# Turning a weight matrix by DMA instead of by TensorE, and one group later

## The chip, the cores and the metric

The kernel runs on one core of a Trainium2 chip. Times are microseconds (us) of device time for one whole execution. The core has TensorE (PE, matrix products and their weight loads), VectorE (DVE), ScalarE (ACT), GpSimd (POOL) and SyncE (SP), each with its own stream of instructions that it runs in order, and 16 DMA engines that all queues share. In this kernel POOL issues the loads and most of the stores, and SP issues the DMA transposes.

## What is computed

```python
def _attn_ref(u, v, z):                    # u, v: 8 x 3072 x 256; z: 8 x 3072 x 64
    scores = (1.0 / S) * np.matmul(z, z.transpose(0, 2, 1))
    attn = np.maximum(scores, 0.0) ** 2
    return u * np.matmul(attn, v)

def _moe_ref(x, w1, w2, w_out):            # w1, w2: 256 x 1024; w_out: 1024 x 256
    g = np.maximum(x @ w1, x @ w2)
    return g @ w_out
```

The second function is applied to the first one's result. Two identities shape the kernel. The score matrix is symmetric, so a block right of the diagonal, turned, is the block left of it. And max(a, b) = max(a - b, 0) + b, so `g @ w_out = relu(x @ (w1 - w2)) @ w_out + x @ (w2 @ w_out)`: the kernel prepares `w15 = w1 - w2` and `W2o = w2 @ w_out` once, and then needs only one wide product, one ReLU and one narrow product for each group.

## The kernel before

**Tiles and groups.** A batch's 3072 rows are 24 tiles of 128; four tiles make a group, six groups a batch. A block is the squared ReLU of the scores of one group against another: 512 x 512 in bf16, held as 128 x 2048 (512 KB) in one of 28 slots (`Block`). A free slot carries a tick from which it counts as free; `release(after=COOL)` sets it 40 ticks on. Scores are made in pairs (`score_pair`): two PE matmuls, two ReLUs out of PSUM (`r_sb`, lines 221 and 223) and a squaring on DVE (lines 229, 231), two pairs to a block. The pairs are numbered in one list. Of batch 0, pairs 0 to 11 are group 0's, 12 to 21 group 1's, 22 to 29 group 2's, 30 to 35 group 3's. For the pairs below 22, every third one gives its second ReLU to DVE rather than ACT.

**Mirrors.** The block (batch, group, block column) right of the diagonal is turned by a DMA transpose on SP (`mirror`, line 262). Most are issued as soon as the block is squared; six of batch 0 go to a list `later` and are issued at set places in groups 1, 2 and 3. SP also turns u (`turn_u`, line 186) and z (`turn_z`, line 142). All of these go through one queue in the order in which the program emits them.

**The start: four plain groups.** Groups 0 to 3 of batch 0 are worked through one by one (the loop over `i`). Each goes over 24 tiles `n` and two halves of v's columns `dc`, two matmuls each (line 278), which is one slot and one tick. At the head of groups 1 to 3 (6, 6 and 9 tiles) and at the tail of groups 0 to 2 (6, 6 and 9) the tiles are taken for one `dc` first and then for the other, else both in turn. New score pairs are emitted every fourth slot (`pair_slots`), ahead of their use. Inside the loop, with `dc` 0, stand the other steps of the start, each at its own `(i, n)`: adding the two halves of the previous group's sums (line 629, groups 1 and 2), its gates (`gate`, line 423: the product with u, times the scale), loading w2, w1 and w_out by POOL (line 646), the later mirrors, and u's and z's transposes.

Into this loop the weights' preparation is laid. At tile 16 of group 2, DVE subtracts `w15`, and PE turns w2 in 16 transposes of 128 x 128 (line 658) into two PSUM tiles, which ACT copies to `w2T_sb` (line 661). At the end of group 2, sixteen matmuls make W2o (line 673), which ACT copies (line 680). PSUM tiles tagged "mm" have four buffers, shared by scores, these products and the feed-forward. `w1`, `w2` and `w2T` lie in three of the 28 slots until they are released.

**After the start.** The sums of group 3 are drained (ACT copies, line 295, and DVE adds, line 297). Then the feed-forward (`ff`) runs for groups 0 and 1: `d_ps` with w15 (line 439), ReLU on ACT (446), `o_ps` first with W2o (453), then with w_out (462). From there couples of groups alternate with the feed-forward of the couple before; couple 2 (groups 4 and 5) uses the mirrored blocks of batch 0, in the order of block columns 4, 5, 2, 3, 0, 1. From batch 1 on, a form with seven instead of eight products is used (line 894), which the change doesn't touch. The schedule is manual: each engine runs its instructions in the order in which the program emits them, and waits are put in where data or a buffer need them.

Of the kernel before, what the change touches and what calls it, by code (L numbers as in the profile page):

```python
# [11 lines left out]
def kernel(  # L12
# [10 lines left out]
    nc = tc.nc  # L23
    fp32 = mybir.dt.float32
    bf16 = mybir.dt.bfloat16
# [7 lines left out]
    P = 128  # L33
# [6 lines left out]
    KD = D // P  # L40
    KF = Dff // P
# [7 lines left out]
    COOL = 40  # L49
# [14 lines left out]
    mm_psum = ctx.enter_context(tc.tile_pool(name="mm_psum", bufs=4, space=bass.MemoryType.PSUM))  # L64
# [56 lines left out]
    def zT_pe(lo, n, engine):  # L121
        tp = mm_psum.tile([P, n, P], bf16, name="tpz", tag="mm")
        for j in range(n):
            nc.tensor.transpose(
                tp[:, j, :], zd_first(lo + j, 1).rearrange("p t h d -> p (t h d)"), ident
            )
        copy = nc.scalar.copy if engine == "act" else nc.vector.tensor_copy
        copy(zT[:, lo : lo + n, :], tp)  # L128
# [144 lines left out]
    def attn_unit(b, g, t, acc, dc, first, last):  # L273
        blk, j = divmod(t, G)
        a = A[b, g, blk]
        for half in range(2):
            rows = ds(half * R, R)
            nc.tensor.matmul(  # L278
                a.out(acc[half, dc]),
                v_at(b, t, dc)[rows],  # L280
                a.moving(rows, j),
                start=first,
                stop=last,
            )
        if dc == KD - 1 and j == G - 1:
            a.release()
# [4 lines left out]
    def drain(acc, dcs):  # L291
        hs = {}
        for dc in dcs:
            hs[dc] = new_h()
            nc.scalar.copy(hs[dc], acc[1, dc])
        for dc in dcs:
            nc.vector.tensor_add(hs[dc], hs[dc], acc[0, dc])
        return hs

    def drain_fast(acc, dc):  # L300
        hs = [new_h() for half in range(2)]
        nc.scalar.copy(hs[1], acc[1, dc])
        nc.vector.tensor_copy(hs[0], acc[0, dc])
        return hs
# [172 lines left out]
    ident = consts.tile([P, P], bf16)  # L477
# [28 lines left out]
    done = 0  # L506
    due = []

    def emit_pair(wait=0):
        nonlocal done  # L510
        early = done < 22
        finish = score_pair(
            *pairs[done], dve_half=1 if early and done % 3 == 0 else None, halves=done == 0
        )
        done += 1
        if wait:
            due.append((tick + wait, finish))
        else:
            finish()
# [10 lines left out]
    def steps_of(i):  # L530
        tiles, both = range(NT), range(KD)
        head = edge(i - 1) if i else 0
        tail = NT - edge(i)
        steps = [(n, dc) for dc in both for n in tiles[:head]]
        steps += [(n, dc) for n in tiles[head:tail] for dc in both]
        return steps + [(n, dc) for dc in both for n in tiles[tail:]]

    def pair_slots(i):
        return (
            [1, 3] + list(range(6, 40, 4)),  # L540
            list(range(3, 41, 4)),
            list(range(3, 41, 4)),
            list(range(0, 44, 4)),
        )[i]

    def need(b, g, n):
        most = pair_at[b, g, 2 * g]
        for t in range(n + 1):
            if t // G >= g:
                most = max(most, pair_at[b, g, t // 2] + 1)  # L550
        return most

    with tc.manual_schedule():
# [14 lines left out]
        w1, w2, w2T = Block(), Block(), Block()  # L568
        w1_sb, w2_sb = (w.ap.rearrange("p (c f) -> p c f", c=KD) for w in (w1, w2))
        w2T_sb = w2T.ap.rearrange("p (c k r) -> p c k r", c=KD, r=P)  # L570

        def new_acc():
            return {
                (half, dc): acc_tile(2 * half + dc) for half in range(2) for dc in range(KD)
            }
# [26 lines left out]
        sums = None  # L602
        for i in range(PLAIN):
            b, g = groups[i]
            if i:
                acc = new_acc()
            new, slots = {}, pair_slots(i)
            for slot, (n, dc) in enumerate(steps_of(i)):
                tick += 1
                k = need(b, g, n)  # L610
                upto = max(k, min(done + 1, k + AHEAD)) if slot in slots else k
                while done < min(upto, len(pairs)):
                    emit_pair()
                if i == 0 and slot in (10, 22):
                    zT_pe(12 if slot == 10 else 20, 8 if slot == 10 else 4, "act")
                    if slot == 22:
                        for x in z_first:
                            x.release()
                attn_unit(b, g, n, acc, dc, n == 0, n == NT - 1)
                if n == NT - 1 and i < PLAIN - 1:  # L620
                    if i < 2:
                        new[dc] = drain_fast(acc, dc)
                    else:
                        new.update(drain(acc, [dc]))
                if dc:
                    continue
                if i in (1, 2) and n in (6, 8):
                    halves = sums[n // 2 - 3]
                    nc.vector.tensor_add(halves[0], *halves)
                    sums[n // 2 - 3] = halves[0]  # L630
                if i and n == 10:
                    gates = gate(*groups[i - 1], sums)
                if i and n in (10, 12):
                    gates.pop(0)()
                if i == 0 and n == 14:
                    turn_u(0, 0)
                if i + 1 < PLAIN:
                    if i and n == 1:
                        load_u(*groups[i + 1])
                    if n == (13 if i == 2 else 16):  # L640
                        turn_u(*groups[i + 1])
                if (i, n) in ((0, 20), (1, 10)):
                    w_in = ((w2_sb, moe_w2), (w1_sb, moe_w1)) if i == 0 else ((w_out_sb, moe_w_out),)
                    nc.vector.memset(w_in[0][0][:, 0, 0:1], 0.0)
                    for w_sb, w in w_in:
                        nc.gpsimd.dma_start(
                            out=w_sb, in_=w.rearrange("(c p) f -> p c f", p=P)
                        )
                if later and n % 4 == 0 and (i == 3 or i and n > 12):
                    later.sort(key=lambda block: block[2])  # L650
                    mirror(*later.pop(0))
                if i == 2 and n == 16:
                    nc.vector.tensor_sub(w15_sb, w1_sb, w2_sb)
                    w1.release()
                    for dc in range(KD):
                        tp = mm_psum.tile([P, KF, P], bf16, name="tpw", tag="mm")
                        for j in range(KF):
                            nc.tensor.transpose(  # L658
                                tp[:, j, :], w2_sb[:, dc, ts(j, P)], ident
                            )  # L660
                        nc.scalar.copy(w2T_sb[:, dc, :, :], tp)
                    w2.release()
                if (i, n) in ((1, 16), (2, 14)):
                    load_z(1, i - 1, held=True)
                if (i, n) == (2, 8):
                    turn_z(1, 0)
                if (i, n) == (3, 14):
                    load_z(1, 2, held=True)
            if i == 2:
                for dc in range(KD):  # L670
                    ps = mm_psum.tile([P, D], fp32, name="w2o_ps", tag="mm")
                    for nb in range(KF):
                        nc.tensor.matmul(  # L673
                            ps,
                            w2T_sb[:, dc, nb, :],
                            w_out_sb[:, nb, :],
                            start=(nb == 0),
                            stop=(nb == KF - 1),
                        )
                    nc.scalar.copy(W2o_sb[:, dc, :], ps)  # L680
                w2T.release()
            sums = new
        sums = None
# [47 lines left out]
        sums = drain(acc, range(KD))  # L731
# [10 lines left out]
        for i in range(PLAIN // 2, len(couples)):  # L742
# [129 lines left out]
            for s, pair in enumerate(steps):  # L872
                while halves_done and halves_done[0][0] <= s:
                    _, name, mm = halves_done.pop(0)
# [13 lines left out]
                for half, (name, w, blk, j) in enumerate(pair):  # L888
                    rows = ds(half * R, R)
                    if name not in acc:  # L890
# [3 lines left out]
                    mm = nc.tensor.matmul(  # L894
                        a.out(acc[name]),
                        w()[rows],
                        a.moving(rows, j),
                        start=name not in opened,
                        stop=left[name] == 0,
                    )  # L900
# [57 lines left out]
```

## Time and profile before

| | us |
|---|---|
| median of 9 runs (lowest, highest) | 911.86 (911.1, 924.36) |
| the profiled execution: its time | 911.63 |
| its span on the core | 909.9 |
| PE busy | 899.1 |
| DVE busy | 724.7 |
| ACT busy | 602.8 |
| POOL busy | 105.6 |
| group 2, by PE's timeline | about 37 to 51.7 |
| group 3, by PE's timeline | 53.55 to 66.4 |
| first feed-forward starts | 66.39 |

The lines of a timeline begin with the start and the duration in us, then engine, line of the kernel, operation, the tiles written and read, their shape, the number of instructions put together in the line, and in brackets the idle time before it and what ended that. "SPq" is SP's queue, where the duration is that of the issue; the landing of a DMA is told apart. Busy PE time counts pipelined matmuls, each 0.2 us behind the next in the steady state, so that durations of single matmuls overlap.

### The profile page before, as it was taken

What the parts mean: (1) busy time and instruction counts of PE and PEld (TensorE: products, weight loads), DVE (VectorE), ACT (ScalarE), POOL (GpSimd) and SP (SyncE); (2) the same over time, 40 slices, a digit from 0 to 9 for tenths busy, and PEclk for the clock granted to TensorE, in tenths of its full rate; (3) what the DMA queues carried; (4) which work ended last, traced back from release to release, by engine and by line L of the source; (5) the groups of instructions that cost most, each with busy time, mean ns of one, the idle gap of its engine ahead of it and who ended that gap; (6) DMA issues with size and microseconds to landing.
All of it is one profiled execution on the core that took longest, in us unless ns stands there. A gap on an engine that the chain in (4) does not pass through costs nothing.

```text
span 909.9 us, 19258 instructions
## 1 busy us (share of the span) xinstructions
PE 899.1 (99%) x7494; PEld 518.4 (57%) x7542; DVE 724.7 (80%) x1095; ACT 602.8 (66%) x1191; POOL 105.6 (12%) x199
## 2 busy tenths in 40 slices
PE   8999999999999999999999999999999999999998
PEld 4456465565565555665646656566465564655655
DVE  6772789779998799887997979978799788995640
ACT  6797966667666676667676666666766567673445
POOL 3101010111110101101011012010110110100000
PEclk9999999999999999999999999999999999999999
DMA  9999999999799896999769999799998999888201
GB/s 186 164 203 211 151 167 173 173 179 171 135 184 182 151 185 115 203 173 168 155 118 214 168 149 173 145 177 150 188 172 141 166 174 184 154 158 147 74 25 70
DMA packets 379500, 145.08 MB, mean 159 GB/s; under 512 B 358160, under 2 KB 362640, under 8 KB 379408
## 3 DMA queue, kind: packets, MB, share of 16 engines
q1 hardware_dynamic: 356960, 91.27, 62.6%
q0 software_dynamic: 22448, 52.57, 30.8%
q8 instruction: 59, 0.97, 0.5%
q14 instruction: 33, 0.27, 0.1%
HBM read 59.77 MB, written 25.17 MB: 93 GB/s over the span
## 4 chain that ended last, share of the span: by engine, by line
PE 97%; DVE 1%; DMA 1%; issue 1%; ACT 0%; ACTq 0%; DVEq 0%; POOLq 0%
PE acc L894 45%; PE o_ps L462 18%; PE d_ps L439 18%; PE s_ps L210 7%; PE o_ps L453 5%; PE acc L278 4%; DMA v_sb<-in_v_dram 1%; DVE blk L231 1%; ACT r_sb L223 0%; PE w2o_ps L673 0%; DVE r_sb L221 0%; ACT zT L128 0%; PE tpw L658 0%; DVE xT L423 0%; ACT o_sb L474 0%
## 5 line engine op out<-in xcount | busy, mean ns | idle before, releaser
L894 PE MATMUL acc<-blk,v_sb 64*128 64x512 bf16 x2208 | 450.4, 376 | 0.0
L223 ACT ACTIVATE r_sb<-s_ps 128x512 bf16<-128x512 f32 (+3 forms) x668 | 334.2, 559 | 122.0 <-PE s_ps L210 78.6
L894 PE MATMUL acc<-blk,vt 64*128 64x512 bf16 x1512 | 364.1, 376 | 0.0
L894 PEld LDWEIGHTS <-v_sb 64*128 64x128 bf16 x2208 | 176.2, 94 | 134.9 <-issue 5.9
L231 DVE TENSOR_TENSOR blk<-r_sb 128x1024 bf16<-128x1024 bf16 x257 | 172.6, 689 | 90.0 <-ACT r_sb L223 89.0
L446 ACT ACTIVATE g_sb<-d_ps 128x512 bf16<-128x512 f32 x384 | 193.3, 630 | 28.2 <-PE acc L894 17.8
L462 PE MATMUL o_ps<-w_out_sb,g_sb 128*128 128x256 bf16 x1536 | 175.5, 273 | 0.0
L894 PEld LDWEIGHTS <-vt 64*128 64x128 bf16 x1512 | 139.2, 94 | 62.4
L439 PE MATMUL d_ps<-xT,w_sb 128*128 128x512 bf16 x720 | 167.6, 379 | 2.6 <-issue 0.2
L462 PEld LDWEIGHTS <-g_sb 128*128 128x128 bf16 x1536 | 150.3, 98 | 17.4
L474 ACT COPY o_sb<-o_ps 128x512 f32<-128x512 f32 (+1 forms) x98 | 56.3, 577 | 132.4 <-PE o_ps L462 132.4
L769 DVE TENSOR_TENSOR h_sb<-h_sb,acc 128x512 f32<-128x512 f32 x168 | 109.4, 682 | 27.7 <-ACT h_sb L773 20.3
L210 PE MATMUL s_ps<-zT 64*128 64x512 bf16 (+3 forms) x676 | 125.8, 357 | 0.6 <-ACT zT L128 0.4
L439 PEld LDWEIGHTS <-w_sb 128*128 128x128 bf16 x768 | 73.2, 98 | 89.7 <-issue 9.9
L475 POOL DMA_DIRECT2D out_dram<-o_sb x88 | 48.1, 546 | 543.8 <-ACT o_sb L474 543.8
L330 DVE TENSOR_TENSOR blk<-blk,blk 128x2048 bf16<-128x2048 bf16 x63 | 76.8, 1219 | 3.7 <-DMA blk<-blk 3.7
L334 DVE TENSOR_TENSOR blk<-blk,blk 128x2048 bf16<-128x2048 bf16 x63 | 77.2, 1225 | 2.2
L784 DVE TENSOR_TENSOR blk<-blk,blk 128x2048 bf16<-128x2048 bf16 x63 | 76.6, 1218 | 0.0
L338 DVE TENSOR_TENSOR blk<-blk,blk 128x2048 bf16<-128x2048 bf16 x63 | 73.4, 1219 | 0.9 <-DMA blk<-blk 0.9
L423 DVE SCALAR_TENSOR_TENSOR xT<-h_sb,uT 128x512 bf16<-128x512 f32 x96 | 62.0, 684 | 3.8 <-PE o_ps L453 3.8
L229 DVE TENSOR_TENSOR blk<-r_sb 128x512 bf16<-128x512 bf16 (+3 forms) x162 | 46.3, 323 | 20.1 <-ACT r_sb L223 19.1
L210 PEld LDWEIGHTS <-zT 64*128 64x128 bf16 x676 | 35.6, 94 | 38.1 <-ACT zT L128 0.9
(50 smaller groups left out, 320.9 us busy)
## 6 DMA issues: line engine op xcount, KB each, us to landing
out_dram<-o_sb POOLq DMA_DIRECT2D x88, 256.0 KB, 3.9
un<-in_u_dram POOLq DMA_DIRECT2D x48, 256.0 KB, 5.8
v_sb<-in_v_dram POOLq DMA_DIRECT2D x21, 512.0 KB, 7.4
blk<-blk SPq DMA_TRANSPOSE x239, 5.0
zn<-in_z_dram POOLq DMA_DIRECT2D x21, 128.0 KB, 4.3
v_sb<-in_v_dram POOLq DMA_DIRECT2D x6, 256.0 KB, 7.6
out_dram<-o_sb SPq DMA_DIRECT2D x6, 256.0 KB, 2.0
blk<-in_moe_w_dram POOLq DMA_DIRECT2D x2, 512.0 KB, 6.5
```

The lines of the kernel that those rows point to most:

```text
L210: nc.tensor.matmul(s_ps[h][:, lo[h] :], zT[rows, z_at(b, blk * G + tiles[h]), :], zT[rows, q + lo[h] // P : q + G, :].rearrange("p t c -> ...
L223: nc.scalar.activation(o, s, AF.Relu)
L231: nc.vector.tensor_mul(a[:, k : k + 2, :], r, r)
L330: nc.vector.tensor_add(*alike(f["S1"], f["A21"], f["A22"]))
L334: nc.vector.tensor_sub(*alike(f["S2"], f["S1"], f["A11"]))
L338: nc.vector.tensor_sub(*alike(f["S3"], f["A11"], f["A21"]))
L439: nc.tensor.matmul(d_ps, w15_sb[:, kc, ts(nb, P)], xT[:, kc, :], start=(kc == 0), stop=(kc == KD - 1),)
L446: nc.scalar.activation(g_sb[:, nb, :], d_ps, AF.Relu)
L462: nc.tensor.matmul(o_ps[t // 2][:, t % 2, :], g_sb[:, nb, ts(t, P)], w_out_sb[:, nb, :], start=False, stop=(nb == KF - 1 and t % 2 == 1),)
L769: nc.vector.tensor_add(out, a, b_)
L784: nc.vector.tensor_sub(f["A12"].ap, f["A12"].ap, f["S2"].ap)
L894: mm = nc.tensor.matmul(a.out(acc[name]), w()[rows], a.moving(rows, j), start=name not in opened, stop=left[name] == 0,)
```

## The change

1. `early` covers pairs below 12 rather than below 22: pairs 12, 15, 18 and 21 give both their ReLUs to ACT.
2. In groups 1 and 2 the first add of halves moves from tile 6 to tile 5, the gates from tiles 10 and 12 to tiles 11 and 14 (groups 1 to 3).
3. The 16 PE transposes of w2 and their two ACT copies at tile 16 of group 2 are gone. In their place SP issues one DMA transpose of the whole w2 at tile 2 of group 3. w2's slot is released there, with 40 ticks to wait, and w2T's one group later.
4. W2o's matmuls and copies stand at the end of group 3 rather than of group 2.

```diff
     def emit_pair(wait=0):
         nonlocal done
-        early = done < 22
+        early = done < 12
...
-                if i in (1, 2) and n in (6, 8):
-                    halves = sums[n // 2 - 3]
-                    nc.vector.tensor_add(halves[0], *halves)
-                    sums[n // 2 - 3] = halves[0]
-                if i and n == 10:
+                if i in (1, 2) and n in (5, 8):
+                    k = n // 8
+                    nc.vector.tensor_add(sums[k][0], *sums[k])
+                    sums[k] = sums[k][0]
+                if i and n == 11:
                     gates = gate(*groups[i - 1], sums)
-                if i and n in (10, 12):
+                if i and n in (11, 14):
                     gates.pop(0)()
...
                 if i == 2 and n == 16:
                     nc.vector.tensor_sub(w15_sb, w1_sb, w2_sb)
                     w1.release()
-                    for dc in range(KD):
-                        tp = mm_psum.tile([P, KF, P], bf16, name="tpw", tag="mm")
-                        for j in range(KF):
-                            nc.tensor.transpose(
-                                tp[:, j, :], w2_sb[:, dc, ts(j, P)], ident
-                            )
-                        nc.scalar.copy(w2T_sb[:, dc, :, :], tp)
-                    w2.release()
+                if (i, n) == (3, 2):
+                    nc.sync.dma_start_transpose(
+                        w2T.ap.rearrange("p (k r) -> p k r", r=P), w2.ap
+                    )
+                    w2.release(after=COOL)
...
-            if i == 2:
+            if i == 3:
                 for dc in range(KD):
                     ps = mm_psum.tile([P, D], fp32, name="w2o_ps", tag="mm")
                     for nb in range(KF):
```

## The prediction

> **What bounds the kernel now.** I read the page first: the busy time of the engines and the chain that ended last.
>
> ```profile
> PE 899.1 (99%) x7494; PEld 518.4 (57%) x7542; DVE 724.7 (80%) x1095; ACT 602.8 (66%) x1191; POOL 105.6 (12%) x199
> PE 97%; DVE 1%; DMA 1%; issue 1%; ACT 0%; ACTq 0%; DVEq 0%; POOLq 0%
> ```
>
> TensorE (PE) is busy for 99% of the span, and 97% of the chain is PE. So a microsecond taken from PE's sequence is gained, one in which PE waits is lost, and other engines count only where PE waits for them. The change lies in the first 80 us, so I next read PE's part of the timeline there (start, duration, engine, line).
>
> ```profile
> 1.19 2.53 PE L581 MATMUL acc<-blk 128*128 128x512 bf16 x7 [1.19 <-DVE blk L557]
> ...
> 32.14 0.37 PE L210 MATMUL s_ps<-zT 64*128 64x512 bf16 x1 [0.20 <-DVE r_sb L221]
> ...
> 32.94 0.82 PE L278 MATMUL acc<-blk,v_sb 64*128 64x512 bf16 x6 [0.21 <-DVE blk L231]
> ...
> 36.15 2.55 PE L278 MATMUL acc<-blk,v_sb 64*128 64x512 bf16 x22 [0.58 <-DVE blk L231]
> ...
> 46.62 1.07 PE L658 MATMUL tpw<-ident,blk 128*128 128x128 bf16 x16
> 47.62 0.82 PE L278 MATMUL acc<-blk,v_sb 64*128 64x512 bf16 x6
> ...
> 51.70 1.92 PE L673 MATMUL w2o_ps<-w_out_sb,blk 128*128 128x256 bf16 x16
> 53.55 0.39 PE L210 MATMUL s_ps<-zT 64*128 64x512 bf16 x2
> ...
> 66.39 3.63 PE L439 MATMUL d_ps<-xT,w_sb 128*128 128x512 bf16 x15
> ```
>
> The 16 transposes hold PE from 46.62 to 47.62 us, 1.00 us; W2o from 51.70 to 53.55, 1.85 us; the first feed-forward starts at 66.39. Group 1 has three waits for VectorE (DVE), 0.20 + 0.21 + 0.58 us.
>
> The new transpose goes through SP's queue, so I read that queue's timeline over groups 2 and 3, then the landing times of its seven L262 transposes issued between 55 and 73 us.
>
> ```profile
> 51.43 2.58 SPq L262 DMA_TRANSPOSE blk<-blk  x1
> 54.11 1.25 SPq L186 DMA_TRANSPOSE uT<-un  x1
> 55.46 18.74 SPq L262 DMA_TRANSPOSE blk<-blk  x7
> 74.30 4.50 SPq L142 DMA_TRANSPOSE zT<-zd  x2
> ```
>
> ```profile
> 65.79 8.41 SPq L262 DMA_TRANSPOSE blk<-blk  x3
> ```
>
> ```profile
> L262 SPq DMA_TRANSPOSE blk<-blk x7: 1809/2341/3511, 55.5 to 71.3; - x7
> DMA to landing us min/median/max: 4.6/5.7/6.2
> ```
>
> SP has no gap: each issue begins where the last one ends, from 51.43 to 78.80 us, at 1.81 to 3.51 us a block. The queue is late. By the program the last seven mirrors are, in order: (0,2,5), (0,0,4), (0,1,4) from group 2, then (0,3,4), (0,0,5), (0,1,5), (0,3,5) from group 3. So (0,0,5), which the program emits at the first tile of group 3 (PE about 53.6 us), is issued only at 65.79: 12 us behind PE. Nobody waits for these seven before couple 2 (groups 4 and 5, after 82 us), so the lag costs nothing today.
>
> **The change part by part.**
>
> *Four ReLUs move.* Pairs 12, 15, 18 and 21 lose their DVE half: 4 x 0.685 us (L221) off DVE, 4 x 0.597 us (L223) onto ScalarE (ACT). From 21.3 to 36.2 us ACT is busy 10.4 of 14.9 us, so 2.4 more fits. With the first add at slot 5 instead of 12 and the gates at slots 22 and 28 instead of 20 and 24, DVE has less to do where PE waits. This takes up to 0.99 us of waits and, where PE's eight-matmul runs stretch from 1.04 to 1.17, 1.17 and 1.34 us, up to 0.56: between 0 and 1.55 us earlier at the end of group 1. I take 1.0. The late gate adds one wait: u's transpose for group 3 is emitted at tile 13 of group 2 and reuses the buffer that the gate at tile 14 still reads. SP comes to it at 54.11, DVE to that gate near 47, so it is free by 7 us; otherwise all of SP's queue would stand behind it.
>
> *The PE transposes go.* PE gets 1.00 us and ACT two copies of 1.03 us, which cost nothing on the path.
>
> *W2o moves* from the end of group 2 to that of group 3: the 16 matmuls and their weight loads keep their 1.85 us and only change place. Its two ACT copies (0.37 us each) now stand ahead of group 3's two drains (0.58 each), which stand ahead of the first feed-forward ReLU. That ReLU starts some 1.5 us after the d_ps matmuls instead of 0.85; with four PSUM buffers at 0.43 us of PE each, the fifth matmul group waits: 0 to 0.8 us, I take 0.6.
>
> *The DMA transpose of w2* is one more instruction in SP's queue, of the size of a block (128 x 2048 bf16, 512 KB), emitted at tile 2 of group 3: after (0,3,4) and (0,0,5), ahead of (0,1,5) and (0,3,5). For those behind it, it costs one more issue, 1.8 to 3.5 us; (0,3,5), now landed at 77.5, and the two z transposes, ended at 78.8, have that room before couple 2. The POOL queue is not touched. w2's and w2T's blocks stay taken for some tens of slots more; the plan has nine or more free through group 3, so no mirror is delayed for lack of one.
>
> But W2o needs it. PE reaches W2o at 66.39 - 1.00 - 1.85 - 1.0 = 62.5 us, and runs in program order: the feed-forward stands behind it. SP reaches the transpose where it now reaches (0,1,5): 65.79 + 3.5 = 69.3 us. The shorter DVE work lets SP start its unbroken run at most 0.6 us sooner, from u's transpose at 33.51, so 68.7. Landing is 4.6 to 6.2 us later in the rows; of those issued from 61 to 66 us it is 4.6, 5.2 and 4.8, and I take 4.8: **w2T lands at 73.5 us, and PE stands idle for 11 us.**
>
> Bounds of the landing: with every mirror from 51.43 on at the fastest issue, 51.43 + 6 x 1.81 + 1.25 + 0.6 (gaps) = 64.2, landed at 68.8; with every one at the slowest, 51.43 + 6 x 3.51 + 1.85 = 74.3, landed at 80.5. The middle rows decide, because this is the same queue in the same stretch.
>
> *PE after the pause.* The first row of PE's timeline shows that PE starts slowly: seven matmuls (five of 512 columns, two of 128) take 2.53 us, where the later rate, 15 of 512 in 3.63, would give about 1.3. This slow rate ends within some 3.3 us of work. Whether 11 us of rest brings it back no row shows: the longest later idle, 0.98 us, does not. So W2o takes between 1.85 and 3.4 us. 11 us is nearer to a start than to 0.98, so I take 3.4.
>
> The Trainium skill, TensorE: Matmul & The Clock Gate, Part 1, says that one idle window of about 3.4 us halves PE's clock, and that about 3.4 us of work brings it back. By it W2o runs wholly at half rate, as I took; by the rows near 0.98 us alone, the sum would be 1.6 us smaller. The skill's DMA: Bandwidth & Descriptors, Anatomy of one DMA, fits 2.0 us plus bytes / 436 GB/s, an estimate of 3.2 us for 512 KB. Counted from tile 2 of group 3 it would have the data there long before PE, and the sum would be a small gain; the rows show that the queue ahead, not the transfer, sets the time.
>
> **Sum.** The feed-forward starts at 73.5 + 3.4 + 0.6 (ACT's order) = 77.5 instead of 66.39: +11.1 us. Everything gained before W2o is swallowed, because the landing decides. From 66 us to the end PE has almost no idle time, so nothing is given back. The profiled execution took 911.63 us (span 909.9 and 1.73 around it): 922.7. The median shown, 911.86, is 0.2 above it: 922.9 us.
>
> **The rivals.**
>
> 1. *The wait is there, but short.* SP's queue runs at its fastest issues, w2T lands at 68.8, W2o takes 1.85 and ACT's order costs nothing: 70.65 instead of 66.39, +4.3, 916.1 us. For it: the issues that start at 61 and 64 us take 2.3 and 2.0 us. Against it: all six rows would have to be at the minimum.
> 2. *The transfer is hidden (not slower).* The transpose is in place when PE comes at 62.5; then PE keeps 1.00 + 1.0 us, less 0.6: 911.86 - 1.4 = 910.5 us, or 909.3 with the whole 1.55 and no loss on ACT. The deciding point is the landing: 62.5 us or before. The six mirrors ahead of it would have to go 11 us sooner; only if SP's issue times were waits on something that this change removes could that be. Up to about 66 us the total would be within 0.5%.
> 3. *A longer stop.* In the trace the queue's data stands still for about 1.3 us near 60 and near 74 us. One such stop ahead of w2T, or the slowest landing (6.2), or slower issues bring it to 77 or later: 926 us and more.
>
> **How the numbers follow.** Main case 0.81, rival 1 0.09, rival 2 0.04, rival 3 0.06. The main case's own range, landing 70.5 to 76.5 with W2o at 1.85 to 3.4: 918 to 926. With the tails cut at about a tenth each side, the range is 917.0 to 926.0. Within 0.5% (4.6 us, about what a measurement of this kernel can tell from no change) lie rival 2 and half of rival 1: 0.08; faster by more than that would need more than all the gains together: 0.01; slower 0.91.
>
> **What would show it.** In the changed kernel PE's longest wait should be that of W2o's first weight load and matmul for a DMA blk<-blk, 8 to 13 us long, starting near 62; SP should issue w2's transpose near 69, directly after the mirror that started near 66; the 16 W2o matmuls after it should take about 3.4 us; group 1's waits for DVE should be gone without any effect on the end. After 80 us the two traces should run alike, shifted by about 11 us. I am wrong if SP comes to that transpose by 60 us, if the queue's issues shorten once PE is ahead, or if PE has work that it can do before W2o.

## The result, and the profile after

| | before | after |
|---|---|---|
| median of all runs, us | 913.36 (52 runs, the 9 above among them) | 922.52 (16 runs) |
| profiled execution: span, us | 909.9 | 920.6 |
| ratio after / before, 95% interval | | 1.0101 (1.0074 to 1.0128) |

The changed kernel is 1.0% slower. Of every version that ran more than once, some executions take 3 to 30 us longer than the rest, and the ratios leave out those more than 1.5% above the version's fastest. The prediction was 922.9 us.

PE's part of the timeline of the changed kernel, at the end of group 3 and after (start, duration, engine, line, and in brackets the idle time before it):

```profile
60.47 1.91 PE L278 MATMUL acc<-blk,v_sb 64*128 64x512 bf16 x16
72.86 3.60 PE L670 MATMUL w2o_ps<-w_out_sb,blk 128*128 128x256 bf16 x16 [10.48 <-DMA blk<-blk]
76.24 0.63 PE L439 MATMUL d_ps<-xT,w_sb 128*128 128x512 bf16 x1
77.10 3.76 PE L439 MATMUL d_ps<-xT,w_sb 128*128 128x512 bf16 x14 [0.22 <-ACT W2o_sb L677]
80.69 1.04 PE L453 MATMUL o_ps<-W2o_sb,xT 128*128 128x256 bf16 x8
```

PE ends group 3 at 62.4 us, 4 us earlier than before, and then stands for 10.48 us until a DMA transpose lands. W2o takes 3.38 us (72.86 to 76.24) instead of 1.85, and from d_ps to o_ps it is 4.45 us instead of 3.48. The o_ps matmuls start 10.8 us later than before. SP's queue in the same stretch shows why:

```profile
54.22 13.59 SPq L262 DMA_TRANSPOSE blk<-blk  x5
67.89 2.45 SPq L656 DMA_TRANSPOSE blk<-blk  x1
70.44 5.18 SPq L262 DMA_TRANSPOSE blk<-blk  x2
79.10 5.66 SPq L142 DMA_TRANSPOSE zT<-zd  x2
```

Line 656 is w2's transpose. It stands behind five mirrors, with gaps of about 0.1 us, and is issued at 67.89; this line's own view has its time to landing:

```profile
L656 SPq DMA_TRANSPOSE blk<-blk x1: 2448/2448/2448, 67.9 to 67.9; - x1
...
DMA to landing us min/median/max: 4.9/4.9/4.9
```

It lands at 72.8, and PE goes on at 72.86. Stretches of the changed kernel (from:to, length, busy time and number of instructions of PE, weight loads, DVE, ACT, POOL, the clock granted to PE, DMA share, GB/s) show PE's clock over the wait:

```profile
62.40:66.00 3.60, 0.00 (x0) 0.00 (x0) 0.07 (x1) 0.00 (x0) 0.00 (x0) 0.81 1.25 271
66.00:72.80 6.80, 0.00 (x0) 0.00 (x0) 0.00 (x0) 0.00 (x0) 0.00 (x0) 0.50 1.04 196
72.80:76.30 3.50, 3.44 (x17) 2.47 (x18) 0.00 (x0) 0.37 (x1) 0.00 (x0) 0.50 1.14 212
76.30:80.70 4.40, 4.18 (x17) 1.79 (x17) 1.69 (x4) 4.21 (x10) 0.00 (x0) 0.78 0.29 56
80.70:84.00 3.30, 3.30 (x32) 2.96 (x31) 1.70 (x4) 1.57 (x4) 0.00 (x0) 1.00 0.29 54
```

The clock falls to half during the wait, and is still half for all of W2o and for some 2 us of the feed-forward.

Couple 2 begins at 82.20 us before and at 92.98 after. From there to the end it is 827.7 and 827.6 us: all of the loss lies ahead of 93 us, and nothing is given back.

### The profile page after: what moved, and what is told of

It reads as the page before. It is cut to its first block, busy times and chain, and to the rows that moved or that the text cites. A ratio compares the mean times of both kernels' runs of the same rounds, so it can differ in the third digit from the quotient of the medians.

```text
span 920.6 us, 19223 instructions
## 1 busy us (share of the span) xinstructions
PE 900.3 (98%) x7478; PEld 520.2 (57%) x7526; DVE 722.1 (78%) x1091; ACT 602.7 (65%) x1193; POOL 105.9 (12%) x199
## 4 chain that ended last, share of the span: by engine, by line
PE 96%; DVE 1%; issue 1%; ACT 1%; SPq 1%; DMA 1%; ACTq 0%; DVEq 0%
PE acc L891 44%; PE o_ps L462 18%; PE d_ps L439 18%; PE s_ps L210 7%; PE o_ps L453 5%; PE acc L278 3%; DVE blk L231 1%; SPq L262 1%; DMA blk<-blk 1%; ACT r_sb L223 1%; PE w2o_ps L670 0%; PE acc L581 0%; PE tpz L124 0%; DVE xT L423 0%; DVE w_sb L653 0%
## 5 line engine op out<-in xcount | busy, mean ns | idle before, releaser
L231 DVE TENSOR_TENSOR blk<-r_sb 128x1024 bf16<-128x1024 bf16 x257 | 172.7, 689 | 89.1 <-ACT r_sb L223 88.3
L891 PEld LDWEIGHTS <-vt 64*128 64x128 bf16 x1512 | 139.2, 94 | 62.4
L439 PEld LDWEIGHTS <-w_sb 128*128 128x128 bf16 x768 | 73.6, 98 | 90.2 <-issue 10.8
```

The lines of the kernel that those rows point to most:

```text
L231: nc.vector.tensor_mul(a[:, k : k + 2, :], r, r)
L439: nc.tensor.matmul(d_ps, w15_sb[:, kc, ts(nb, P)], xT[:, kc, :], start=(kc == 0), stop=(kc == KD - 1),)
L891: mm = nc.tensor.matmul(a.out(acc[name]), w()[rows], a.moving(rows, j), start=name not in opened, stop=left[name] == 0,)
```

## The experiments

Spans of single profiles also hold waits that come and go between executions, so I read from each profile when PE comes to certain points, in us from the start:

| kernel | w2T landed | W2o starts | d_ps starts | o_ps starts | couple 2 starts | span |
|---|---|---|---|---|---|---|
| before | - | 51.70 | 66.39 | 69.87 | 82.20 | 909.9 |
| after | 72.8 | 72.86 | 76.24 | 80.69 | 92.98 | 920.6 |
| wait_gone | 72.8 | 64.30 | 66.05 | 70.11 | 82.45 | 913.5 |
| mid_turn | 67.4 | 67.48 | 70.87 | 74.99 | 87.31 | 923.0 |
| warm_wait | 71.3 | 72.45 | 74.20 | 78.26 | 90.59 | 918.2 |
| early_turn | 52.6 | 62.74 | 64.50 | 68.56 | 80.90 | 909.6 |
| drain_first | 72.1 | 72.14 | 75.44 | 78.90 | 91.18 | 918.8 |
| early_drain | 54.6 | 63.31 | 65.06 | 68.52 | 80.80 | 928.9 |

**The wait taken away (wait_gone).**

```diff
-                            w2T_sb[:, dc, nb, :],
+                            w2_sb[:, dc, ts(nb, P)],
```

(w2's slot is released at the end of group 3.)

> W2o's matmuls read w2 as it lies instead of w2T, so that they don't wait for the DMA transpose; the transpose is still issued at the same place, with all its load on the queue. This changes the computation: W2o is then a product with unturned 128x128 pieces. Theory (PE's wait for the landing is the whole loss): PE goes on at 62.4 us, W2o takes 1.85 us, the first feed-forward's o_ps matmuls start near 68.3 instead of 80.7, span 908.2 us. Rival (the transpose slows the other transfers, or the moved ReLUs and W2o's place cost time by themselves): the span stays above 912.

PE went through W2o without a wait, in 1.75 us, while the transpose landed at 72.8 as in the changed kernel. The feed-forward started 10 us earlier than after; it would have been about 12, but this execution lost 2 us at its start, 1.6 of them in a wait for v's first load. So the wait was the loss. The span, 913.5, missed the expected 908.2, and the waits of PE in this profile say where:

```profile
PE s_ps L210 <- DMA zT<-zd: 3.2, 2, 2.7
PE acc L278 <- DMA v_sb<-in_v_dram: 1.6, 1, 1.6
```

The columns are the total wait, how often, and the longest. A new wait: the scores of the next batch, near 100 us, for z's transposes. I come back to it.

**Two places earlier in the queue (mid_turn).**

```diff
-                if (i, n) == (3, 2):
+                if (i, n) == (2, 22):
                     nc.sync.dma_start_transpose(
```

> The changed kernel with w2's transpose two places earlier in SP's queue (tile 22 of group 2, ahead of the mirrors (0,3,4) and (0,0,5)). Theory (the place in the queue sets the landing, some 2.3 to 2.8 us a place): issue near 62.4, landing near 67.2, PE idle 4.8 instead of 10.5 us, W2o still slow (3.4), span 914.8. Rival (the transfer itself or its waits are slow, whatever its place): landing stays near 72.8, span 920.6.

```profile
62.97 2.97 SPq L656 DMA_TRANSPOSE blk<-blk  x1
```

```profile
67.48 3.59 PE L670 MATMUL w2o_ps<-w_out_sb,blk 128*128 128x256 bf16 x16 [4.93 <-DMA blk<-blk]
```

These are SP's queue and PE's timeline of that kernel. Two places are 4.9 us of issue (67.89 less 62.97) and 5.4 us of landing, PE's wait falls to 4.93 us, and couple 2 starts 5.7 us earlier, as expected. The place in the queue sets the landing, not the transfer, which takes 4.5 us here and 4.9 in the changed kernel. The span missed its 914.8, because this execution lost 6 us near 242 us, behind a late load of v, and 2 more towards the end.

**PE kept busy in the wait (warm_wait).**

```diff
             if i == 3:
+                warm_ps = mm_psum.tile([P, GW], fp32, name="warm_ps", tag="mm")
+                for _ in range(46):
+                    nc.tensor.matmul(
+                        warm_ps, w15_sb[:, 0, :P], w15_sb[:, 0, :GW], start=True, stop=True
+                    )
```

> The changed kernel with 46 matmuls of 128x512 on w15 into a spare PSUM tile ahead of W2o, which fill the wait (46 x 0.216 = 9.9 us) and are read by nobody. Theory (after the rest PE runs at half clock): the landing stays near 72.9, W2o takes 1.85 instead of 3.4 us and the first d_ps run is shorter too, span 918.7. Rival (W2o is slow because of the DMA traffic or its place): W2o stays at 3.4, span 920.6 or more.

```profile
62.52 10.10 PE L669 MATMUL warm_ps<-w_sb 128*128 128x512 bf16 x45
72.45 1.91 PE L675 MATMUL w2o_ps<-w_out_sb,blk 128*128 128x256 bf16 x16
74.20 1.89 PE L439 MATMUL d_ps<-xT,w_sb 128*128 128x512 bf16 x7
76.30 2.06 PE L439 MATMUL d_ps<-xT,w_sb 128*128 128x512 bf16 x8 [0.21 <-ACT g_sb L446]
```

In PE's timeline of this kernel W2o starts 0.4 us earlier and takes 1.75 us, with the clock at 1.00 throughout; the span is 918.2, expected 918.7. So the half clock cost 1.6 us in W2o and about 0.4 in the feed-forward. Work that nobody reads made the kernel 2.4 us faster, since the wait was long enough to halve PE's clock. The rest of the longer d_ps run, 4.06 instead of 3.48 us, stays and ends on ScalarE: that is the order on ACT.

**The order on ScalarE (drain_first, early_drain).** Group 3's drain stands ahead of W2o in the program; in early_drain w2's transpose is early as well.

```diff
             if i == 3:
+                last = drain(acc, range(KD))
                 for dc in range(KD):
...
-        sums = drain(acc, range(KD))
+        sums = last
```

> The changed kernel with group 3's drain ahead of W2o in the program, so that ScalarE copies the sums during the wait and has only W2o's two copies ahead of the first feed-forward ReLU. If ScalarE's order stretches the first d_ps run (4.45 us to the o_ps matmuls, 3.48 before), it falls to 3.5 to 3.7 and the span to 919.7; if the half clock does, it stays near 4.4 and the span at 920.6.

> The transpose at tile 7 of group 2 and group 3's drain ahead of W2o, together. Here PE is at full clock, so the order on ScalarE shows alone: with the drain behind W2o's copies the first d_ps run should take 0.6 us more than 3.48, with the drain ahead of them not; span 0.6 us below that of the version with the early transpose alone, 907.6. Rival: no difference.

With the drain first, d_ps to o_ps takes 3.46 us in both (75.44 to 78.90, 65.06 to 68.52), against 4.06 at full clock with the drain behind (early_turn). In drain_first the clock came back at about 75.4, just ahead of the d_ps run, so there the two reasons can't be told apart; in early_drain PE never rested before W2o, and 0.6 us is the order's price. Its rows:

```profile
65.06 3.62 PE L439 MATMUL d_ps<-xT,w_sb 128*128 128x512 bf16 x15
68.52 1.04 PE L453 MATMUL o_ps<-W2o_sb,xT 128*128 128x256 bf16 x8
```

But early_drain's span was 928.9, and its median of 12 runs 924.69, against 914.25 for the kernel before in the same comparison; the ratio is 1.0016 (0.9943 to 1.009), from three of the 12. PE's waits in its profile:

```profile
PE s_ps L210 <- DMA zT<-zd: 10.3, 1, 10.3
PE s_ps L210 <- ACT o_sb L474: 3.6, 1, 3.6
```

**The transpose hidden (early_turn).** The place is `(2, 7)`, behind the last mirror that group 3 needs.

> The changed kernel with w2's transpose at tile 7 of group 2, right behind the mirror (0,2,3), the last that group 3 needs. Theory: issue near 48.5, landing near 54, hidden from PE, which comes to W2o at 62.4; span 908.2, time 910, faster than before by 0.2%. The mirrors behind it come 2.4 us later and nobody waits for them before 82 us. Rival (the extra 512 KB in a full queue hurts someone else): a new PE wait on a mirror in group 3 or couple 2, span 911 or more.

w2T landed at 52.6 us, and nobody waited for it. Couple 2 started 1.3 us earlier than before; my rival 2 had given 1.4. The span was 909.6 instead of 908.2. PE kept its lead to the end: its last matmul ends at 904.6 us, before at 905.9. The further us lies behind ScalarE's last copy, where only the last stores are under way. Over 12 runs the ratio to the kernel before is 1.0016 (0.9978 to 1.0054): no gain that can be measured. Its times go from 910.1 to 941.5, and half of them are above 923. With the transpose ahead, z's go out later in a queue that is behind anyway. SP's queue in its profile:

```profile
47.77 3.09 SPq L656 DMA_TRANSPOSE blk<-blk  x1
...
56.19 20.13 SPq L262 DMA_TRANSPOSE blk<-blk  x7
76.41 6.47 SPq L142 DMA_TRANSPOSE zT<-zd  x2
82.98 8.43 SPq L186 DMA_TRANSPOSE uT<-un  x2
```

Here z's two transposes took 7.6 and 9.8 us to land (84.0 and 88.3). PE comes to them near 88 and 97 us, where its waits for them begin in early_drain and too_early, so they came 4 and 9 us ahead of it.

**Earlier still (too_early).** The place is `(2, 2)`, ahead of the mirror that group 3 reads at its ninth tile.

> The changed kernel with w2's transpose at tile 2 of group 2, ahead of the mirror (0,2,3) that group 3 reads at its ninth tile. Theory (each place costs the one behind it about 2.3 us): w2T is hidden, but the mirror lands near 54 instead of 51.8, PE waits some 2.3 us in group 3 near 51.7, span 910.5. Rival (the queue has room there): no wait, span 908.2.

The theory was wrong, and the rival right only on the wait. The mirror landed at 52.2, since SP got through its first mirrors faster in this execution (w2's transpose was issued at 43.8), and PE waited 0.2 us for it instead of 2.3. Couple 2 started at 80.84, like early_turn's. The span, 927.1, again comes from later waits, the first of them for z:

```profile
PE s_ps L210 <- DMA zT<-zd: 3.8, 1, 3.8
PE acc L891 <- DVE blk L334: 3.1, 4, 1.1
PE s_ps L210 <- ACT o_sb L474: 2.3, 1, 2.3
```

**The scores' part alone (relus_only).** The kernel before with parts 1 and 2 of the change.

> The kernel before with the first two parts alone: pairs 12 to 21 with both ReLUs on ScalarE, adds at tiles 5 and 8, gates at 11 and 14; w2 is turned by PE and W2o stands at the end of group 2 as before. Theory: PE's waits for VectorE in group 1 go, span 908.6 (909.9 less 1.35, the lead that the changed kernel has over the one before in group 2). Rival (the waits move to ScalarE or to another place): span 909.9 or more.

Group 1's three waits for DVE are gone, and two new ones of 0.3 and 0.2 have come. The span is 909.2: 0.7 us less, half of what I expected; 0.4 of the rest is a later start of group 1 in this execution. A span alone can't show a gain of this size: before_late (below), which is the kernel before up to 82 us, is also 0.7 us ahead of it, by an earlier start of group 1 (20.45 us against 21.11). Ratio 0.9984 (0.9945 to 1.0024): no difference that can be measured.

**What is last in the queue (z_ahead, before_z).** In z_ahead, on top of early_drain, and in before_z, on top of the kernel before, z's transposes go ahead of the mirror (0,1,5):

```diff
+                if (i, n) == (3, 2):
+                    load_z(1, 2, held=True)
+                if (i, n) in ((3, 3), (3, 18)):
+                    turn_z(1, 1 if n == 3 else 2)
-                if later and n % 4 == 0 and (i == 3 or i and n > 12):
+                if later and n % 4 == 0 and (i == 3 and n in (0, 20) or i in (1, 2) and n > 12):
```

(The two calls of `turn_z` behind the first feed-forward are gone.)

> The changed kernel with w2's transpose at tile 7 of group 2, group 3's drain ahead of W2o, and z's two transposes for the next batch drawn ahead in SP's queue: z's last load at tile 2 of group 3, its transposes at tiles 3 and 18 of group 3, ahead of the mirror (0,1,5), which moves to tile 20. Theory (with w2T hidden, the added 2.4 us in SP's queue pushes z's transposes into the time of v's loads, where they land late and PE waits in couple 2): z lands before 80, no wait for zT at 87 to 101, couple 2 starts near 80.3 and the span is 907.9, and its runs scatter no more than those of the kernel before. Rival (those waits come from elsewhere, or the mirrors now become the late ones): a wait in couple 2 remains, or the runs scatter as with the two versions that turn w2 early.

> The kernel before with z's transposes drawn ahead alone. Its profiled execution has no wait for zT, so the span should stay at 909.9. If late z transposes are also behind the longer runs of the kernel before, its runs scatter less than those of the kernel before; if those come from other places (waits of PE near 242, 314 or 800 us in other profiles), they scatter alike.

The theory fell in part. Couple 2 no longer waits for z, but now the mirror at the end of the queue is late. Its line, first in z_ahead's profile, then in before_z's:

```profile
L262 SPq DMA_TRANSPOSE blk<-blk x1: 6326/6326/6326, 78.6 to 78.6; - x1
...
  PE acc L894: 0.5, 1
...
DMA to landing us min/median/max: 24.1/24.1/24.1
```

```profile
L262 SPq DMA_TRANSPOSE blk<-blk x2: 1584/7688/13793, 71.9 to 76.3; - x2
...
  PE acc L896: 14.8, 1
...
DMA to landing us min/median/max: 5.0/23.6/42.1
```

One mirror took 24 us, another 42, and in before_z PE waited 14.8 us for it, the longest wait of this study and in a kernel without w2's transpose. (z_ahead's other waits, 3.7 us for z near 176 us among them, belong to later batches.) So it isn't z's transposes that are slow; it is whatever SP's queue still holds after 80 us. Ratios 1.0067 (1.0024 to 1.011) and 1.0005 (0.997 to 1.0041). before_z scatters like the kernel before: 7 of its 12 runs are above 914 us, and 15 of 23.

**The loads moved away (late_loads, before_late).** At that time POOL starts two loads of v (512 KB each) at the beginning of couple 2. They move to steps 30, 36 and 60, once on top of early_drain and once alone.

```diff
-                    (2, load_v, 1, 0),
+                    (30, load_v, 1, 0),
-                    (6, load_v, 1, 1),
-                    (34, load_v, 1, 2),
+                    (36, load_v, 1, 1),
+                    (60, load_v, 1, 2),
```

> The version with w2's transpose at tile 7 of group 2 and group 3's drain ahead of W2o, and v's three loads in couple 2 moved from steps 2, 6 and 34 to steps 30, 36 and 60 (about 88, 90 and 96 us). Theory (whatever is left in SP's queue when v's loads start is held up for 10 to 40 us, and the added transpose leaves more of it there): z's and u's transposes land before 90, no wait of PE for a DMA in couple 2, couple 2 starts near 80.3, span 907.9, and most runs lie within 2 us of each other, like those of the changed kernel, whose loads came after the queue was empty. Rival (the hold-up has another source): zT or a mirror lands near 98 or later again and PE waits for it, and the runs scatter over 20 us as before.

> The kernel before with v's three loads at the same later steps, and nothing else. Theory: the span of an undisturbed execution stays at 909.9, and the runs above 914 us (about half of those of the kernel before) become rare. Rival: they scatter as those of the kernel before.

In late_loads z landed at 83.5 and 87.6, u's two transposes at 88.3 and 89.2, and PE had no wait for a DMA in couple 2. But its span was 915.4, since another load, of the next batch's v, came late near 231 us and held DVE, then PE:

```profile
DVE vt L170 <- DMA v_sb<-in_v_dram: 4.6, 1, 4.6
```

Its 12 runs still go from 909.2 to 931.7, ratio 1.0011 (0.9974 to 1.0048). The best three, 909.2 to 909.8, lie 1.1 to 1.8 us below the fastest of the kernel before in that comparison, 910.9, near the 1.4 that the prediction gave for a hidden transpose; most runs don't reach them. By the medians of all their runs the four versions with the transpose at tile 7 that ran 12 times (early_turn, early_drain, z_ahead, late_loads) are 7.5, 10.4, 7.9 and 5.4 us above the kernel before in the same comparison. One profile of each can't show where most of the longer runs lose this; it stays open.

before_late shows the hold-up itself, in one profile of each kernel. The landing of u's two transposes, issued near 84 us, first in the kernel before, then in before_late:

```profile
L186 SPq DMA_TRANSPOSE uT<-un x2: 1232/1257/1282, 82.6 to 84.3; - x2
...
DMA to landing us min/median/max: 5.3/8.8/12.3
```

```profile
L186 SPq DMA_TRANSPOSE uT<-un x2: 1233/1476/1718, 83.7 to 85.2; - x2
...
DMA to landing us min/median/max: 4.0/4.2/4.5
```

The mirror behind them takes 5.8 us instead of 19.3. That the hold-up also makes the longer runs of the kernel before is likely, but not shown. For it: 11 of before_late's 12 runs lie between 910.95 and 911.67 us, against 11 of 23 of the kernel before below 912 in the same comparison. Against it: relus_only, whose loads are not moved, has only 2 of 12 runs above 914, against 12 of 23 of the kernel before in its comparison, and none of the longer runs of the kernel before was profiled. The fastest run is the same, 910.95 against 910.92, and the ratio 0.998 (0.995 to 1.0009). No version here beats the kernel before by more than the measurement can tell.

## Why the prediction was right

| step | predicted | measured |
|---|---|---|
| PE comes to W2o, us | 62.5 | 62.4 |
| SP issues w2's transpose | 68.7 | 67.9 |
| from issue to landing | 4.8 | 4.9 |
| w2T lands | 73.5 | 72.8 |
| W2o takes | 3.4 | 3.38 |
| ACT's order | 0.6 | 0.6 (early_turn against early_drain) |
| feed-forward later by | 11.1 | 10.8 (at o_ps) |
| time | 922.9 | 922.5 |

*The wait.* The step that carried the forecast was to see that SP's queue, unbroken from 51 to 79 us, ran 12 us behind PE, and to place the new transpose in it by the program's order. wait_gone shows that PE's wait was the loss, mid_turn that the place in the queue sets it: 2.5 us a place. The 3.2 us that the prediction estimated for the transfer alone are too short, w2's transpose took 4.9 us: the Trainium skill, DMA: Bandwidth & Descriptors, Anatomy of one DMA, gives that fit for DMAs issued from GpSimd, and this one is issued by SP.

*The clock.* I took W2o at half rate from the first row of PE's timeline, since 11 us of rest was nearer to the start than to 0.98 us. The granted clock of the changed kernel, 0.50, and warm_wait show it. The rule of the Trainium skill, TensorE: Matmul & The Clock Gate, Part 1, that I had set beside it agrees in kind (half rate after a pause), but its times of about 3.4 us differ from those measured: the clock fell 2.2 us after PE's last matmul and came back 5.4 us after its restart. Two terms were off and partly cancelled: the landing was 0.7 us earlier, and the slow clock lasted beyond W2o, 0.4 us in the feed-forward, which I had put at nothing.

*How near it came.* That the time was met to 0.4 us is in part luck. In the four versions that leave w2's transpose at tile 2 of group 3, SP comes to it at 67.9 (after), 67.8 (wait_gone), 67.4 (drain_first) and 66.5 us (warm_wait); and in the kernel before it comes to the mirror (0,1,5), from whose place the forecast was worked out, at 69.4 in one profile and at 68.4 in another (before_late). So the 0.7 us of the landing lie within what one execution differs from the next. The 922.9 also counts from the median of the nine runs shown; against the median of all 52, 913.36, the change costs 9.2 us, since 25 of these 52 are above 914 us. The prediction's third rival is added up too high: a stop of 1.3 us or the slowest landing brings 73.5 to 74.8 or 74.9, and both together to 76.2; only slower issues on top of them reach 77.

*What is swallowed.* PE did gain ahead of W2o: it ended group 3 4.1 us earlier, W2o's 1.85 among them. None of it is in the time, as predicted. In relus_only and early_turn, where it isn't swallowed, it is 0.7 (1.1 from the start of group 1) and 1.3 us.

*The hidden transfer.* Rival 2 did not occur, and its price was right at couple 2. What I had wrong stands in the change's part on the DMA transpose: that those behind it lose one issue, 1.8 to 3.5 us, and have that room. The 78.8 that it gave for the end of z's transposes is the end of their issue. In the kernel before they land 8.4 and 7.8 us after it begins, at 82.7 and 85.0, when couple 2 (82.2) and v's loads (83.8) have begun: there was no room. In the changed kernel it holds because PE is 11 us late, so that z's transposes land 3.0 and 3.1 us after their issue, by 86.6, before couple 2 (92.98) starts v's loads. Where PE doesn't wait, as in wait_gone, early_drain and too_early, z's transposes or the mirror ahead of them meet these loads, and PE waited 2.7, 10.3 and 3.8 us for z.

## What to carry to other kernels

Work moved from an engine to a DMA queue starts when the queue comes to it, not where the program has it: read how far the queue is behind at that place (here 12 us) before asking how long the transfer takes (here 4.9). A wait of several microseconds on PE costs its length and a slow start after it, 1.6 to 2.0 us here (drain_first, after). And a queue that just gets done before a burst of loads is at its limit, even if no engine waits for it in the profile: one more transfer of 2.4 us there can turn into a wait of ten.

## What was not expected of the hardware

- Transposes in SP's queue that were still under way when POOL's loads of v started took up to 24 and 42 us to land (z_ahead, before_z), where 4.6 to 6.2 is usual for a mirror. The kernel before has one such too (19.3 us, issued at 86 us), for which no engine waits; with the loads some 7 us later (before_late) the same mirror takes 5.8 us.
- The clock fell to half 2.2 us (after), 2.4 us (too_early) and 2.8 us (mid_turn) after PE's last matmul, and a rest of 2.7 us (wait_gone) left it at 1.00. It came back 3.2 us (drain_first), 4.7 us (mid_turn) and 5.4 us (after, too_early) after PE's restart. These times differ because the clock changes in steps that don't start with PE's rest: in every trace of this case the stretches between two changes last whole multiples of 3.41 us. At half clock they are 3.41 us (mid_turn, 246.29 to 249.70), 6.83 (drain_first, 68.52 to 75.35), 10.24 (early_drain, 91.30 to 101.54) and 13.65 (after, 64.60 to 78.25). How much rest within a step halves the clock these traces don't settle: in wait_gone 1.6 us near 7 us did, followed by half clock from 8.13 to 11.54, and the 2.7 us near 100 us didn't; counted on from 11.54 in steps of 3.41 us, one ends at 100.3, in the middle of that rest.
